# An S5 scan and an H3 convolution in one single-core kernel: parameter loads issued by ScalarE, and a written-out order of 758 operations replaced by another

## The chip, the core and the metric

The kernel runs on one core of a Trainium2 chip. A core has five engines with a queue each, which run side by side and wait for each other through semaphores: TensorE (PE; its weight loads are shown as PEld), VectorE (DVE), ScalarE (ACT), GpSimd (POOL) and SyncE (SP, which here does nothing but issue DMAs). PE writes into PSUM, which has 8 banks; ACT and DVE carry results from PSUM to SBUF ("evictions"). The metric is the device time of one execution in microseconds, as the median of several runs.

## The reference, cut to what matters

```python
# part A, columns 0..639 of the output
Lam_bar = jnp.exp(dt * Lam)                                # dt = exp(log_dt), Lam = Lambda_re + i Lambda_im
Bu = jnp.einsum("bld,pd->blp", x, ((Lam_bar - 1) / Lam)[:, None] * Bmat)
for t in range(L):                                         # L = 2048, 640 states
    h = Lam_bar * h + Bu[:, t, :]
y = 2.0 * jnp.einsum("blp,dp->bld", hseq, Cmat).real + x * Dskip
# part B, columns 640..1279
kv = causal_conv4(k, shift_k) * v                          # 4 taps along the sequence
y = irfft(rfft(kv, 4096) * rfft(ssm_k, 4096))[:2048]       # per channel
out_B = q * (y + kv * ssm_D)
```

All tensors are bf16; both parts have 2048 positions and 640 channels.

## The kernel before: how the work is staged and ordered

`build` lists some 758 operations, most of them a single engine instruction or one group of matmuls. `Program.depend` derives what each must wait for from the memory it reads and writes. `Program.emit` (L135) then issues them in the order of the string `ORDER` (L1050): `48V0` is operation 48 on DVE with bank 0. Letters are T for PE, A for ACT, V for DVE, G for POOL, S for SP. Each engine runs its own operations in this order, and an operation that waits holds everything behind it on that engine. A matmul group also waits until the operation that last read its PSUM banks is done; most groups use two banks, so four of them fit.

Part A splits the sequence into 128 blocks of 16 and builds the scan by a tree. In the code and below the operations are named so:

- `ld_par` (L346) loads Lambda and log_dt, `t_par` (L354) turns them, and a chain of small operations makes the tables (`rn`, `fr`, `fi`, `al`, `cf`, `rr`, `gm`). `ld_Braw` loads the first piece of B, `turn_B` (L499) turns it and `ev_B` (L504) evicts it; `ld_B1`, `ld_B2` (L489) and `ld_x` (L522) load by transposing DMAs.
- `up2`, `up1`, `up0` (L554, L575) are the large matmuls of the tree, evicted at L571, L595 and L620. `gC` (L544) scales C, evicted at L548. `cs_*` (L636 to L660) is the scan over the blocks: two halves h = 0, 1, each a chain of two swaps on PE (`cs_v`, `cs_k`) and six DVE operations that ends in `cs_h` (L660).
- `dn` (L677, L679) and `ad` (L695 on ACT, L697 on DVE) go down the tree. When `ad` runs on ACT, PE first adds the old value by a matmul with an identity (L677).
- `C0` to `C15` (L714) project 128 rows each, 20 matmuls; `ev_C` (L716, DVE) adds `xd` (L706) and `st_A` (L720) stores.

Part B takes two halves of 320 channels (hf = 0, 1). Its Fourier transform is done in matmul steps:

- For each of five blocks of 128 channels, `ld_k` and `ld_v` load transposed, and `cm`, `ca`, `cx` (L197 and L198, L795, L796) do the four taps. There is one buffer for k, so that `ld_k1` waits for the last `cm0`. `pl` (L802) stores the block, and `rl` (L812) reads it back in another layout.
- `ld_h` (L762) and `ld_D` (L750) load the filter of one half and its skip weight, and `addD` (L764) adds them. The filter of half 1 lands in memory that the block scan `cs_*` uses, so that its four loads wait for `cs_h` of the second half. `s1` (L832, evicted at L837) and `s2` (L850, evicted at L863) transform filter (`s1h`, `s2h`) and data (`s1k`, `s2k`). `pp`, `pq`, `py`, `pz` (L874 to L881) form the product. `r2` (L895, evicted at L900) and `r1` (L916, evicted with the factor q at L928, DVE) go back. `r1` needs the tables `g_m`, `g_q`, `g_s`, `g_k` (L324 to L333).
- `warm0` and `warm1` (L514) are four matmuls each, whose result nobody reads.

ACT computes exponentials and sines from function tables and loads another table when the kind changes. In the trace such a load carries the line of the operation behind it.

Of the kernel before, what the change touches and what calls it, by code (L numbers as in the profile page):

```python
# [20 lines left out]
PACT, PDVE, PPOOL, PPE, PSP = "A", "V", "G", "T", "S"  # L21
# [314 lines left out]
def params(c):  # L336

    P, nc, v, f = c.P, c.nc, c.v, c.f
# [4 lines left out]
    P.add("pr0", {V: .15}, lambda e: e.memset(pr, 0.0), outs=[pr])  # L343
    for k, src in enumerate((lam_re, lam_im, ldt_in)):
        rows = pr[10 * k:10 * k + 10, :]
        P.add("ld_par", {PSP: .1}, lambda e, rows=rows, src=src: e.dma_start(  # L346
            out=rows.rearrange("p (a b) -> p a b", a=2), in_=bass.AP(src.tensor, 0, [[64, 10], [0, 2], [1, 64]])),
            outs=[tk[:, k:k + 1]], ins=[pr], nbytes=2560)
    c.DR = v("DR")
# [597 lines left out]
def build(c):  # L947

    setup(c)
    params(c)  # L950
    a, b = PartA(c), PartB(c)
    c.a, c.b = a, b
# [78 lines left out]
def plain_order(P):  # L1031
# [16 lines left out]


ORDER = (  # L1050
# [36 lines left out]
)  # L1087


# [67 lines left out]
```

## Time and profile before

| | |
|---|---|
| runs | 208.45 us median of 3, 206.47 to 208.98 |
| profiled execution | span 205.6 us from first to last instruction; no other time of it is given |
| busy share of the span | PE 88%, DVE 81%, ACT 69%, POOL 37% |
| chain that ended last | PE 46%, ACT 24%, DVE 10%, DMA 10%, no wait shown 5% |
| ACT function table loads | 6 of 1.283 us |

The profile comes from one execution. In its pages a row of the timeline has the start in us, the duration, the engine (ACTq and SPq are the issue of a DMA by ACT or SP), the line, the operation, the tiles, and the count; in square brackets stands how long the engine was idle before it and what released it. `acc` is PSUM and `arena` is the one SBUF tile in which all data lie. A row of groups ends with the busy time and the mean ns of one. The view of stretches gives, for each stretch of the span, the busy time of each engine and the granted clock of PE (1.00 is full speed).

### The profile page before, as it was taken

What the parts mean: (1) busy time and instruction counts of PE and PEld (TensorE: products, weight loads), DVE (VectorE), ACT (ScalarE), POOL (GpSimd) and SP (SyncE); (2) the same over time, 40 slices, a digit from 0 to 9 for tenths busy, and PEclk for the clock granted to TensorE, in tenths of its full rate; (3) what the DMA queues carried; (4) which work ended last, traced back from release to release, by engine and by line L of the source; (5) the groups of instructions that cost most, each with busy time, mean ns of one, the idle gap of its engine ahead of it and who ended that gap; (6) DMA issues with size and microseconds to landing.
All of it is one profiled execution on the core that took longest, in us unless ns stands there. A gap on an engine that the chain in (4) does not pass through costs nothing.

```text
span 205.6 us, 8247 instructions
## 1 busy us (share of the span) xinstructions
PE 180.7 (88%) x3713; PEld 118.7 (58%) x3713; DVE 166.2 (81%) x228; ACT 142.5 (69%) x164; POOL 76.4 (37%) x63
## 2 busy tenths in 40 slices
PE   2399999999999989768759999999999998999891
PEld 0245444554556647447546757546577776887670
DVE  4929349798949698798697989999999899988821
ACT  2628897887994889999738799996999950550000
POOL 8799900000040727037310180684910507120120
PEclk9999999999999999999965899999999999999998
DMA  4999979989999989659948990140962794166866
GB/s 124 160 195 168 183 163 168 136 187 156 228 222 180 267 135 199 109 100 129 134 141 171 161 101 3 40 129 3 212 80 67 171 218 96 66 160 168 227 165 156
DMA packets 107549, 30.20 MB, mean 147 GB/s; under 512 B 102394, under 2 KB 106874, under 8 KB 107514
## 3 DMA queue, kind: packets, MB, share of 16 engines
q1 hardware_dynamic: 107226, 29.35, 77.4%
q8 instruction: 29, 0.48, 1.1%
q10 hardware_dynamic: 288, 0.33, 0.5%
q14 instruction: 6, 0.05, 0.1%
HBM read 10.99 MB, written 7.86 MB: 92 GB/s over the span
## 4 chain that ended last, share of the span: by engine, by line
PE 46%; ACT 24%; DVE 10%; DMA 10%; issue 5%; POOL 1%; SPq 0%; DVEq 0%; ACTq 0%
PE acc L714 14%; PE acc L554 12%; ACT arena L863 8%; ACT arena L837 7%; DMA arena<-in_B_k_dram 6%; PE acc L850 5%; PE acc L679 3%; PE acc L832 3%; PE acc L895 3%; DVE arena L716 2%; PE acc L575 2%; DVE arena L874 2%; ACT arena L198 2%; DVE arena L877 2%; PE acc L916 2%
## 5 line engine op out<-in xcount | busy, mean ns | idle before, releaser
L554 PE MATMUL acc<-arena 128*64 128x512 bf16 x400 | 50.0, 403 | 3.9 <-issue 3.6
L714 PE MATMUL acc<-arena 128*128 128x320 bf16 x320 | 46.0, 300 | 1.4 <-DVE arena L716 0.8
L554 PEld LDWEIGHTS <-arena 128*64 128x64 bf16 x400 | 23.4, 112 | 26.5 <-issue 6.5
L714 PEld LDWEIGHTS <-arena 128*128 128x128 bf16 x320 | 30.4, 98 | 14.4 <-issue 0.9
L837 ACT CAST arena<-acc 128x1024 bf16<-128x1024 f32 x34 | 32.7, 1033 | 5.8 <-PE acc L832 5.6
L863 ACT CAST arena<-acc 128x960 bf16<-128x960 f32 (+1 forms) x37 | 32.5, 907 | 5.7 <-PE acc L850 4.9
L850 PE MATMUL acc<-arena 128*64 128x160 bf16 x512 | 23.2, 238 | 2.5 <-ACT arena L863 1.3
L832 PE MATMUL acc<-arena 64*64 64x64 bf16 x1280 | 18.2, 205 | 6.9 <-ACT arena L837 3.0
L706 POOL TENSOR_TENSOR arena<-arena 128x640 bf16<-128x640 bf16 x9 | 13.4, 1499 | 28.0 <-DMA arena<-in_A_x_dram 28.0
L850 PEld LDWEIGHTS <-arena 128*64 128x64 bf16 x512 | 18.2, 111 | 8.8 <-ACT arena L863 3.7
L900 ACT CAST arena<-acc 128x1024 bf16<-128x1024 f32 x16 | 15.5, 1021 | 10.8 <-PE acc L895 10.8
L832 PEld LDWEIGHTS <-arena 64*64 64x64 bf16 x1280 | 14.5, 117 | 14.0 <-ACT arena L837 6.2
L795 DVE TENSOR_TENSOR arena<-arena 128x2048 bf16<-128x2048 bf16 x14 | 17.8, 1268 | 5.8 <-ACT arena L198 5.5
L198 ACT ACTIVATE arena<-arena 128x2048 bf16<-128x2048 bf16 (+3 forms) x15 | 18.6, 1243 | 5.4 <-DMA arena<-in_B_k_dram 4.2
L697 DVE TENSOR_TENSOR arena<-acc,arena 128x1024 bf16<-128x1024 f32 (+2 forms) x17 | 19.2, 1148 | 1.4 <-ACT arena L863 0.7
L881 POOL TENSOR_TENSOR arena<-arena 128x1280 bf16<-128x1280 bf16 x3 | 8.5, 2821 | 27.5 <-DVE arena L877 27.5
L716 DVE TENSOR_TENSOR arena<-acc,arena 128x640 bf16<-128x640 f32 x16 | 13.3, 832 | 4.9 <-PE acc L714 4.8
L434 POOL TENSOR_TENSOR arena<-arena 128x1280 bf16<-128x1280 bf16 x1 | 2.3, 2331 | 32.1 <-ACT arena L198 32.1
L679 PE MATMUL acc<-arena 128*128 128x512 bf16 (+2 forms) x50 | 13.0, 346 | 0.6 <-ACT arena L837 0.5
L197 DVE TENSOR_SCALAR arena<-arena 128x2048 bf16<-128x2048 bf16 (+2 forms) x17 | 11.8, 699 | 1.2 <-DMA arena<-in_B_k_dram 0.9
L928 DVE TENSOR_TENSOR arena<-acc,arena 128x960 bf16<-128x960 f32 (+1 forms) x12 | 11.9, 1040 | 0.7 <-DMA arena<-in_B_q_dram 0.4
L874 DVE TENSOR_TENSOR arena<-arena 128x2560 bf16<-128x2560 bf16 x8 | 11.9, 1486 | 0.1
(139 smaller groups left out, 269.1 us busy)
## 6 DMA issues: line engine op xcount, KB each, us to landing
out_dram<-arena SPq DMA_DIRECT2D x32, 160.0 KB, 3.1
arena<-in_B_ssm_k_dram SPq DMA_DIRECT2D x8, 320.0 KB, 7.1
kv_rows<-arena SPq DMA_DIRECT2D x5, 512.0 KB, 4.2
arena<-kv_rows SPq DMA_DIRECT2D x8, 320.0 KB, 5.6
arena<-in_A_x_dram SPq DMA_DIRECT2D x16, 160.0 KB, 4.2
arena<-in_B_q_dram SPq DMA_DIRECT2D x8, 320.0 KB, 5.7
arena<-in_A_B_im_dram ACTq DMA_DIRECT2D x1, 160.0 KB
arena<-in_A_B_re_dram ACTq DMA_DIRECT2D x1, 160.0 KB, 2.7
```

What stands on the lines that cost most here:

```text
L198: self.SM = {nc.scalar: lambda out, in_, by: nc.scalar.mul(out, in_, by), nc.vector: vm(nc.vector), nc.gpsimd: vm(nc.gpsimd)}
L554: e.matmul(o[64 * r:64 * r + 64], lhsT=self.BT[j][:, r, d, :], rhs=self.XP[:, d, 2 * q:2 * q + 2], start=(d == 0), stop=(d == 4), skip_gro ...
L679: e.matmul(B[:, o:o + 128 * k], lhsT=c.RR[:, n, j, :], rhs=A[:, j, q:q + k, 0:128], start=not by_pe, stop=True, skip_group_check=True)
L697: e.tensor_tensor(out=o, in0=b, in1=o, op=ALU.add)
L714: e.matmul(B[:, 512 * b:512 * b + 320], lhsT=lh[j], rhs=self.CT[:, j, 320 * b:320 * b + 320], start=(j == 0), stop=(j == 9))
L716: P.add(f"ev_C{i}", {PDVE: dve(640)}, lambda e, B: e.tensor_tensor(out=ys.rearrange("p (b n) -> p b n", b=2), in0=B.rearrange("p (b n) -> ...
L795: P.add(f"ca{d}_{j}", tt, lambda e: e.tensor_tensor(out=t1, in0=t1, in1=t2, op=ALU.add), outs=[t1], ins=[t1, t2])
L832: e.matmul(B[64 * b:64 * b + 64, 512 * l + 64 * i:512 * l + 64 * i + 64], lhsT=lh[i][ps], rhs=F[ps, b, :], start=True, stop=True, tile_pos ...
L837: P.add(f"e1{what}{hf}_{u}", {PACT: act(1024), PDVE: dve(1024)}, lambda e, B: c.CP[e](out=out, in_=B.rearrange("p (l n k s) -> p k s l n", ...
L850: e.matmul(B[64 * s:64 * s + 64, 512 * b + 160 * i:512 * b + 160 * i + 160], lhsT=c.W[:, k, 64 * b:64 * b + 64], rhs=self.AS[hf][:, k, 160 ...
L863: c.CP[e](out=out, in_=b.rearrange("p r (k j n) -> p r k j n", k=n, j=4) if nj > 1 else b.rearrange("p r (k x) -> p r k x", k=n))
L874: P.add(f"pp{hf}", n1, lambda e: e.tensor_tensor(out=pt, in0=X, in1=Yk, op=ALU.mult), outs=[pt], ins=[X, Yk])
```

## The change

The function of `ld_par` is on ACT instead of SP, and the whole string `ORDER` is new. No operation is added, removed or altered.

```diff
-        P.add("ld_par", {PSP: .1}, lambda e, rows=rows, src=src: e.dma_start(
+        P.add("ld_par", {PACT: .1}, lambda e, rows=rows, src=src: e.dma_start(
...
 ORDER = (
-    "48V0 33G0 50S0 123A0 51S0 115G0 122A0 108G0 42G0 49S0 6G0 72G0 7V0 73G0 137S0 1G0 18G0 0G0 30G0 2V0 119G0 8V0 114S0 12V0 465G0 "
...
-    "721V4 658T0 722S0 754V0 662T4 755T6 659V0 535S0 676S0 663V4 661V2 738S0 745T0 756V6 667S0 757S0 674S0 677S0 739G0 666S0 740T4 "
-    "665S0 746V0 747S0 664S0 120T2 741V4 742S0"
+    "114S0 48V0 72G0 42G0 115G0 33G0 6G0 18G0 73G0 83V0 8V0 9V0 12V0 122A0 7V0 27V0 25V0 136S0 0G0 11V0 19V0 26V0 269V0 1G0 2V0 "
+    "120T5 458V0 43V0 3V0 10V0 24V0 28V0 29V0 50A0 49A0 51A0 53T4 54V4 87V0 86V0 15G0 34G0 123A0 124T5 55A0 56V0 125A5 63V0 14V0 "
...
+    "664S0 739V0 740T6 741V6 742S0 744G0 745T3 746V3 747S0"
 )
```

By the names above, the two orders differ so:

| engine | before | after |
|---|---|---|
| SP, start | ld_par x3, x7, ld_sk, B1, x6, B1, k0, B2, B2, x5, x4 | ld_sk, x6, x7, B1, B1, x4, x5, B2, B2, k0 |
| ACT, start | ld_Braw, ld_Braw, dt, rn, rn, ev_B, f1_s | ld_Braw, ld_par x3, ld_Braw, dt, ev_B, rn x4, f1_s |
| PE, start | t_par, warm1, turn_B, up21_0 | warm0, t_par, turn_B, up21_0 |
| PE, around the block scan | cs_v0, 8 other groups and 6 of s2h0, cs_k0, 2 of s2h0, cs_v1, 3 of s2h0 and 3 of s1k0, cs_k1 | cs_v0, 8 other groups and 2 of s2h0, cs_k0, 2 of s2h0, cs_v1, 5 of s2h0, cs_k1, 2 of s2h0, warm1, s1k0 |
| PE, between s2k0 and s2h1 | 11 of s2k0 and C0 ahead of the first s1h1 | 7 of s2k0, dn2_0, dn2_9, dn2_5 ahead of the first s1h1; C0 after the seventh s1h1 |
| PE, end | r21 x10, C14, r11 x3, C8, r11 x3, C15, C13, C12, warm0 | C8, then r21 mixed with r10, r11 x3, C15, r11 x3, C14, C12, C13 |
| POOL | addD on DVE; 9 of xd | addD0 and addD1; 6 of xd |

91 operations have another engine: 3 `ld_par` from SP to ACT; 37 from DVE to ACT (10 evictions of 1024 columns at L571, L837 and L900, 9 at L863, 5 `ad`, 5 smaller evictions at L548 and L620, 3 taps `cm`, 3 `cf`, 2 `g_k`); 32 from ACT to DVE (13 evictions of 1024 columns, 9 at L863, 2 `ad`, 2 smaller ones, 6 taps `cm`); 8 from DVE to POOL (5 products, 2 `addD`, 1 `xd`), 9 from POOL to DVE (5 products, 4 `xd`), and 2 from POOL to ACT. By ORDER, exponentials and sines on ACT alternate so that four table loads are needed in place of six. All eight `g_k` stand on ACT (five before). `ad` stands on ACT seven times (four before). All eleven evictions of `s2h0` stand on ACT (eight before).

66 rows, old and new, of the table ORDER are left out of this document.

## The prediction

> **What bounds the kernel now.** I read the share of each engine first, then the stretches between places where PE visibly stops, then the timeline around the two longest stops.
>
> ```profile
> core 0: us, PE busy (x) PEld busy (x) DVE busy (x) ACT busy (x) POOL busy (x), PEclk, DMA share, GB/s
> 0.00:10.67 10.67, 2.96 (x16) 1.65 (x16) 7.74 (x40) 5.34 (x8) 8.39 (x24) 1.00 0.78 143
> 10.67:76.00 65.33, 64.16 (x966) 35.22 (x966) 48.20 (x69) 51.15 (x61) 21.74 (x19) 1.00 1.07 183
> 76.00:101.30 25.30, 20.36 (x633) 15.51 (x635) 22.18 (x25) 23.94 (x31) 10.25 (x5) 1.00 0.85 133
> 101.30:104.70 3.40, 0.90 (x46) 0.63 (x40) 2.27 (x3) 1.02 (x2) 2.36 (x1) 1.00 1.15 304
> 104.70:114.90 10.20, 8.88 (x313) 6.59 (x314) 9.02 (x9) 7.72 (x9) 0.00 (x0) 0.50 0.54 118
> 114.90:150.00 35.10, 33.71 (x684) 21.66 (x684) 33.10 (x35) 30.61 (x35) 21.47 (x10) 1.00 0.54 91
> 150.00:175.00 25.00, 24.23 (x420) 18.20 (x417) 23.68 (x31) 16.80 (x18) 7.38 (x4) 1.00 0.62 124
> 175.00:200.40 25.40, 24.71 (x650) 19.05 (x648) 19.18 (x21) 5.89 (x6) 4.82 (x4) 1.00 0.62 158
> ```
>
> PE is the bound from 10.67 to 76 us (64.16 of 65.33) and from 114.9 to 200.4. In 76 to 101 ACT is (23.94 of 25.30): PE waits there for evictions. Two losses remain. PE's large matmuls start only at 10.67. And PE does next to nothing from 101.3 to 104.7 (0.90 of 3.40, a share of 26%), after which its granted clock is 0.50 for the next 10.2 us.
>
> ```profile
> 102.44 1.60 DVE L764 TENSOR_TENSOR arena<-arena 128x80 bf16<-128x80 bf16 x1 [1.51 <-DMA arena<-in_B_ssm_D_dram]
> 104.13 0.44 PE L832 MATMUL acc<-arena 64*64 64x64 bf16 x32 [2.37 <-DVE arena L764]
> 89.27 0.49 DVE L660 TENSOR_TENSOR arena<-arena 128x640 bf16<-128x640 bf16 x1
> 89.91 8.05 SPq L762 DMA_DIRECT2D arena<-in_B_ssm_k_dram  x4
> 98.07 1.23 SPq L750 DMA_DIRECT2D arena<-in_B_ssm_D_dram  x1
> ```
>
> The stop at 101.3 is a chain: cs_h of the second half ends at 89.76 (L660), the four loads of half 1's filter go out from 89.91, addD1 runs at 102.44 and frees PE at 104.13. So the end of the block scan, and 12.7 us of loading behind it, set when s1h1 can begin.
>
> **The change, part by part.**
>
> *The start.*
>
> ```profile
> 0.94 0.41 SPq L346 DMA_DIRECT2D arena<-in_A_Lambda_im_dram  x1
> 1.75 0.33 SPq L346 DMA_DIRECT2D arena<-in_A_Lambda_re_dram  x1
> 2.12 1.57 SPq L522 DMA_TRANSPOSE arena<-in_A_x_dram  x1
> 3.74 0.58 SPq L745 DMA_DIRECT2D arena<-in_B_shift_k_dram  x1
> 5.74 1.80 SPq L522 DMA_TRANSPOSE arena<-in_A_x_dram  x1
> DMA to landing us min/median/max: 3.9/4.9/5.1
> 7.10 1.23 ACT L504 COPY arena<-acc 128x1280 bf16<-128x1280 bf16 x1 [0.38 <-PE acc L499]
> 10.67 1.92 PE L554 MATMUL acc<-arena 128*64 128x512 bf16 x8 [3.60 <-issue]
> ```
>
> The first large matmul waits for two pieces of x. The second is issued at 5.74 and lands 4.9 later (the landing row is that of L522), at 10.6; ev_B, its other condition, was done at 8.33. After, SP issues ld_sk (0.58) and the two pieces (1.80 and 1.57) first. From about 0.75 the second goes out at 0.75 + 0.58 + 1.80 = 3.1 and lands at 8.0. Three parameter loads and one of B leave its front. On ACT they stand ahead of the second ld_Braw and move that by their 0.94 to 2.08, 1.1 us. They themselves go out as early as on SP; but warm0 now stands ahead of t_par on PE, and its four matmuls cost t_par, dt and so ev_B some 0.2 to 0.5 us: ev_B ends near 8.5. PE starts at 8.5 in place of 10.67: **-2.2 us** (between -1.5, if warm0's input is late by 0.7, and -2.6, where x alone decides). PE has work without a pause behind it, so this carries through to 76.
>
> *The block scan and the filter of half 1.* After, four of the s2h0 groups that stood ahead of cs_k0 stand behind it, the three DVE evictions between the two halves go to ACT, and the scan no longer queues behind them. I walked the chain with the durations of the rows: cs_v0 at 70.8, cs_k0 at 76, cs_v1 at 78.1, cs_k1 at 82.8, cs_h ends near 84.6, 5 us earlier than 89.76. Loads and addD1 (on POOL, where no row shows this size: 0.2 by POOL's 1.5 for 640 columns at L706, row below, 1.6 if it runs as DVE's did) end near 98. PE reaches s1h1 near 99.5, so that the stop of 2.37 goes: -2.4. What is late next is ACT, which feeds PE in this stretch.
>
> *The half clock.* It followed a stretch of 3.4 us with PE at 26%; 76 to 101 with 20.36 of 25.30 (80%) kept clock 1.00. Without the stop I take it to stay away: of 10.2 us, 7.72 are ACT's work, so that at full clock up to 2.5 go: -2.5. By the bounds: nothing if it comes anyway, and -4.4, half of PE's 8.88, if ACT kept up.
>
> *Work moved between engines.*
>
> ```profile
> L837 ACT CAST arena<-acc 128x1024 bf16<-128x1024 f32 x34 | 32.7, 1033 | 5.8 <-PE acc L832 5.6
> L863 ACT CAST arena<-acc 128x960 bf16<-128x960 f32 x29 | 27.4, 966 | 4.1 <-PE acc L850 3.3 <-ACT arena L620 0.2
> L863 DVE CAST arena<-acc 128x960 bf16<-128x960 f32 x7 | 8.1, 1153 | 1.0 <-PE acc L850 0.5 <-ACT arena L620 0.4
> L837 DVE CAST arena<-acc 128x1024 bf16<-128x1024 f32 x6 | 7.2, 1222 | 3.9 <-PE acc L832 3.9
> L198 ACT ACTIVATE arena<-arena 128x2048 bf16<-128x2048 bf16 x6 | 12.0, 2002 | 5.2 <-DMA arena<-in_B_k_dram 4.2 <-DVE arena L795 1.0
> L197 DVE TENSOR_SCALAR arena<-arena 128x2048 bf16<-128x2048 bf16 x14 | 10.7, 768 | 1.1 <-DMA arena<-in_B_k_dram 0.9
> L877 DVE TENSOR_TENSOR arena<-arena 128x1280 bf16<-128x1280 bf16 x14 | 11.2, 821 | 0.2
> L877 POOL TENSOR_TENSOR arena<-arena 128x1280 bf16<-128x1280 bf16 x2 | 5.2, 2615 | 3.5 <-DVE arena L874 3.4
> L198 ACT ACTIVATE arena<-arena 128x1024 bf16<-128x1024 bf16 x5 | 5.7, 1154 | 0.0
> L366 ACT ACT_TABLE_LOAD x2 | 2.6, 1283 | 0.0
> L863 ACT CAST arena<-acc 128x640 bf16<-128x640 f32 x8 | 5.5, 693 | 1.7 <-PE acc L850 1.5
> L706 POOL TENSOR_TENSOR arena<-arena 128x640 bf16<-128x640 bf16 x9 | 13.4, 1499 | 28.0 <-DMA arena<-in_A_x_dram 28.0
> L900 ACT CAST arena<-acc 128x1024 bf16<-128x1024 f32 x16 | 15.5, 1021 | 10.8 <-PE acc L895 10.8
> ```
>
> Over the whole run the moves cancel. ACT gives up 13 x 1.03 and 6 x 2.0 and gets 10 x 1.03, 3 x 2.0 and a net three more `ad` (1.0) and three g_k (1.15): nil within 1 us, less two table loads (2.6). DVE gets three more evictions of 1.22 and three more taps of 0.77, and gives three `ad`, two g_k, addD and some smaller ones: 1 to 2 us less. The products change places one for one (0.82 on DVE, 2.6 on POOL). POOL loses three xd and one g_k, 6 us of time it had to spare. It is the place that counts. In 76 to 101, three s2h0 evictions come to ACT and one e1k0 leaves: 2 x 0.97 = **+1.9** on the engine that bounds. With the two terms above the middle gives -2.4 - 2.5 + 1.9 = **-3.0 us**.
>
> From 101 on ACT gets three more g_k (3.5), three more `ad` (3.0) and one table load (1.3), and hands 3 evictions of 640 columns to DVE (-2.1): some 5.7 us against the idle time it has from 101.3 to 150, which is 48.7 - 39.35 = 9.3. That hides it, barely. Two costs stay on PE. `ad` on ACT needs identity matmuls: four more of 512 columns behind s2h1, by C's 20 matmuls of 320 columns in 2.89 (row below) 0.23 each, +0.9. And the first r11 group now follows ten r21 groups, eight of whose evictions (1.02) stand on ACT, with C14 no longer between: r21 pairs leave PE faster than ACT empties them, +1.5 by my walk (0 if DVE's two finish early, 2.9 if all of C14's cover is missed). **+2.4 us.**
>
> ```profile
> 98.06 2.89 PE L714 MATMUL acc<-arena 128*128 128x320 bf16 x20
> 53.19 1.83 ACT arena L837 x2
> 55.04 1.28 ACT L452
> 56.33 1.27 ACT arena L452
> ```
>
> The table load of 1.28 begins as the eviction before it ends (53.19 + 1.83 = 55.02) and the sine follows at once. [...]
>
> DMA loads of x, C and k behind the start are covered: SP's k1 still waits for the last cm0 (DVE, about 28 as before), and k2 for cm1_0. The moved stores and r loads have 3 us or more to spare except r9 and r10, whose xd stand on DVE near 167: a miss there costs up to 1 us, and is in the range.
>
> **Sum.** -2.2 - 3.0 + 2.4 = -2.8 on a span of 205.6: 202.8. The median of the runs, 208.45, is 2.85 above the profiled span; I add that: **205.65**, said as 205.7.
>
> **Rivals.**
>
> *Nothing missed (faster).* Without the +2.4 (the idle time takes the identity matmuls, the r11 wait does not come) the sum is -5.2: 203.3. For it speaks that PE, from 114.9 on, leaves only 2.9 us unused now (85.5 less 82.65 busy) and has the same groups to run; against it, that ACT has 5.7 us more to do there than it had.
>
> *ACT takes the place (no change).* After 101 its spare 9.3 us are not in one place: where PE runs a C (2.89) ACT idles, and then cannot catch up. If half of the spare is out of reach, 5.7 - 4.7 = 1.0 more is on the path, and if none of it can be used 5.7: then -2.8 + 5.7 = +2.9 at most, 211.3; halfway 208.5. For it: g_k and er20 all precede the first r10 group. Against: 10.8 us of ACT's idle time stood among the evictions of r2 (row of L900) and can take the late g_k.
>
> *Half clock again (slower).* The new order leaves PE short pauses between groups while ACT evicts, in 84 to 101 some 60% to 65% busy by my walk, between the 26% that lost the clock and the 80% that kept it. If the clock drops there, the 10.2 us at 0.50 fall on C0 and the groups about it in full: -2.5 is not gained and C0's 2.89 doubles, -2.8 + 2.5 + 2.9 = +2.6, 211.0; if it drops once more in the PE-bound part, half of 10.2 comes on top: 216. The point from which it makes the kernel slower by 2% is a second drop. [...]
>
> *The parameter loads do nothing by themselves.* They free 1.14 us of SP; ld_B1's place between the two x's frees more. That is in the -2.2.
>
> **How the numbers follow.** The likeliest case, 202.5 to 208 by its own bounds, has 0.50; nothing missed 0.20; ACT 0.17 (208.5); half clock 0.13 (211 to 216). Within 2% of 208.45, about what a measurement of this kernel can tell from no change, lie 204.3 to 212.6. Faster: the second case and a fifth of the first, 0.30. Slower: half of the last, a little of the third and some for what I don't see, 0.12. Same: 0.58. The range, 202.3 to 211, leaves out less than 2 in 10.
>
> **What would show it.** Right: the first L554 matmul near 8.5; the second L660 near 85 and the four L762 loads at once behind it; no stop of PE over 2 us near 100; clock 1.00 from the first microseconds to the end; a pause of 1 to 2 us ahead of the first r11 group (L916). Wrong: a stretch of 0.50 in the middle; ACT without idle time from 76 to the last g_k and PE waiting for it; DVE waiting for the loads of L705.

## The result, and the profile after

| | before | changed |
|---|---|---|
| median of the runs, us | 207.64 (206.47 to 208.98, 4 runs) | 220.81 (217.71 to 221.99, 4 runs) |
| ratio, with its 95% interval | | 1.056 (1.045 to 1.067) |
| profiled execution: span, own time | 205.6, not known | 219.7, 221.48 |

The change makes the kernel 5.6% slower, some 12 us (the medians differ by 13). All ratios here are of the faster executions of either kernel, and the profiled execution of the changed one is among the longer of its four. First the stretches of its profile, cut near the places where those of before were cut.

```profile
core 0: us, PE busy (x) PEld busy (x) DVE busy (x) ACT busy (x) POOL busy (x), PEclk, DMA share, GB/s
8.92:76.00 67.08, 64.28 (x981) 34.91 (x986) 51.13 (x62) 42.98 (x65) 23.16 (x24) 1.00 1.12 186
76.00:101.30 25.30, 17.31 (x512) 12.41 (x508) 18.53 (x23) 19.77 (x24) 7.00 (x3) 0.87 0.94 112
101.30:114.90 13.60, 10.91 (x357) 8.06 (x354) 11.70 (x13) 11.31 (x14) 4.15 (x3) 1.00 0.59 123
114.90:150.00 35.10, 27.37 (x692) 17.58 (x688) 32.23 (x27) 26.79 (x29) 16.78 (x7) 0.90 0.57 107
```

From 76 to 101 both PE and ACT have idle time now (ACT 19.77 of 25.30, where it had 23.94): neither bounds. From 115 to 150 PE, the bound before (33.71 of 35.10), works 27.37; DVE has 32.23. So PE waits for something new in two places. The list of what PE waits for (us in total, times, longest) names them:

```profile
PE acc L832 <- issue: 6.0, 4, 3.1
PE acc L679 <- DVE arena L716: 4.9, 1, 4.9
...
PE acc L850 <- DVE arena L863: 1.7, 1, 1.7
PE acc L714 <- DVE arena L716: 1.5, 1, 1.5
...
PE acc L916 <- ACT arena L900: 1.1, 1, 1.1
```

The two largest were not there before: 6.0 us at the s1 groups (L832) in which PE waits for nothing that the profile shows, and 4.9 us in one piece for ev_C3 (L716). In the list of the kernel before no matmul of L679 waits for L716, and two short waits stand there, behind the start, for nothing that the profile shows:

```profile
PE acc L714 <- issue: 0.6, 1, 0.6
...
PE acc L832 <- issue: 0.3, 1, 0.3
```

The second place first, in the timelines of DVE, POOL and PE around it:

```profile
130.41 4.70 DVE L877 TENSOR_TENSOR arena<-arena 128x1280 bf16<-128x1280 bf16 x3
135.14 3.11 DVE L881 TENSOR_TENSOR arena<-arena 128x1280 bf16<-128x1280 bf16 x1
138.17 0.48 DVE L706 TENSOR_TENSOR arena<-arena 128x640 bf16<-128x640 bf16 x1
138.78 0.82 DVE L716 TENSOR_TENSOR arena<-acc,arena 128x640 bf16<-128x640 f32 x1
```

```profile
131.37 3.06 POOL L881 TENSOR_TENSOR arena<-arena 128x1280 bf16<-128x1280 bf16 x1 [1.85 <-DVE arena L877]
134.38 3.19 POOL L879 TENSOR_TENSOR arena<-arena 128x1280 bf16<-128x1280 bf16 x1
```

```profile
139.66 0.61 PE L679 MATMUL acc<-arena 128*128 128x512 bf16 x1 [4.92 <-DVE arena L716]
```

A product takes DVE 0.82. Here three of them take 4.70 and the next one 3.11: DVE's third L877 ends 0.7 us after POOL's first product does (131.37 + 3.06 = 134.43), and its L881 ends 138.25, 0.7 after POOL's second (137.57). They did not work for 3 us, they stood until POOL was done. All of it lies in front of ev_C3, whose PSUM bank dn1_6 needs.

The other place, PE's timeline near 93, where the changed order runs the s1k0 groups (32 matmuls each) one behind the other:

```profile
92.93 0.28 PE L832 MATMUL acc<-arena 64*64 64x64 bf16 x11 [0.46 <-ACT arena L837]
96.31 1.55 PE L832 MATMUL acc<-arena 64*64 64x64 bf16 x117 [3.09 <-issue]
```

PE stops for 3.09 us behind the eleventh of the 32 matmuls of s1k0_8. A wait of this program stands ahead of a group's first matmul, never inside a group.

### The profile page after: what moved, and what is told of

The parts are those of the page before. It is cut to its first block, busy times and chain, and to the rows that moved or that the text cites. A ratio compares the mean times of both kernels' runs of the same rounds, so it can differ in the third digit from the quotient of the medians.

```text
span 219.7 us, 8254 instructions
## 1 busy us (share of the span) xinstructions
PE 184.0 (84%) x3712; PEld 118.9 (54%) x3715; DVE 174.0 (79%) x224; ACT 138.8 (63%) x169; POOL 71.7 (33%) x60
## 4 chain that ended last, share of the span: by engine, by line
PE 62%; ACT 13%; DVE 13%; issue 7%; DMA 2%; ACTq 1%; DVEq 0%
PE acc L554 22%; PE acc L714 15%; ACT arena L863 7%; PE acc L850 5%; PE acc L575 4%; PE acc L832 4%; PE acc L679 4%; PE acc L895 4%; DVE arena L877 3%; ACT arena L837 3%; DVE arena L863 2%; PE acc L916 2%; DVE arena L716 2%; ACT arena L900 2%; DVE arena L881 2%
## 5 line engine op out<-in xcount | busy, mean ns | idle before, releaser
L714 PE MATMUL acc<-arena 128*128 128x320 bf16 x320 | 45.4, 299 | 2.8 <-DVE arena L716 1.5
L714 PEld LDWEIGHTS <-arena 128*128 128x128 bf16 x320 | 30.6, 98 | 15.2 <-DVE arena L716 1.6
L863 ACT CAST arena<-acc 128x960 bf16<-128x960 f32 (+1 forms) x37 | 33.2, 929 | 8.1 <-PE acc L850 7.4
L837 ACT CAST arena<-acc 128x1024 bf16<-128x1024 f32 x31 | 30.1, 1021 | 11.4 <-PE acc L832 11.4
L850 PE MATMUL acc<-arena 128*64 128x160 bf16 x512 | 24.1, 243 | 6.2 <-ACT arena L863 2.5
L850 PEld LDWEIGHTS <-arena 128*64 128x64 bf16 x512 | 19.0, 114 | 13.2 <-ACT arena L863 4.7
L900 ACT CAST arena<-acc 128x1024 bf16<-128x1024 f32 x18 | 17.8, 1016 | 12.3 <-PE acc L895 12.2
L832 PE MATMUL acc<-arena 64*64 64x64 bf16 x1280 | 16.9, 201 | 8.0 <-issue 6.0
L832 PEld LDWEIGHTS <-arena 64*64 64x64 bf16 x1280 | 13.7, 114 | 15.1 <-issue 8.5
L679 PE MATMUL acc<-arena 128*128 128x512 bf16 (+2 forms) x50 | 15.4, 390 | 5.5 <-DVE arena L716 4.9
L697 DVE TENSOR_TENSOR arena<-acc,arena 128x1024 bf16<-128x1024 f32 (+1 forms) x14 | 16.1, 1164 | 4.2 <-PE acc L679 3.2
L877 POOL TENSOR_TENSOR arena<-arena 128x1280 bf16<-128x1280 bf16 x4 | 10.4, 2612 | 27.7 <-DVE arena L874 27.7
L198 ACT ACTIVATE arena<-arena 128x1024 bf16<-128x1024 bf16 (+3 forms) x16 | 15.9, 1017 | 4.7 <-DMA arena<-in_B_k_dram 3.1
L795 DVE TENSOR_TENSOR arena<-arena 128x2048 bf16<-128x2048 bf16 x14 | 17.1, 1220 | 1.5 <-ACT arena L198 1.1
L716 DVE TENSOR_TENSOR arena<-acc,arena 128x640 bf16<-128x640 f32 x16 | 13.0, 821 | 6.6 <-PE acc L714 6.0
L197 DVE TENSOR_SCALAR arena<-arena 128x2048 bf16<-128x2048 bf16 x17 | 15.2, 905 | 0.4
L837 DVE CAST arena<-acc 128x1024 bf16<-128x1024 f32 x9 | 10.9, 1218 | 4.6 <-PE acc L832 4.5
L706 POOL TENSOR_TENSOR arena<-arena 128x640 bf16<-128x640 bf16 x6 | 8.4, 1399 | 18.4 <-DMA arena<-in_A_x_dram 18.4
L877 DVE TENSOR_TENSOR arena<-arena 128x1280 bf16<-128x1280 bf16 x12 | 13.1, 1111 | 0.2
```

Of the source, the lines that this page charges most:

```text
L679: e.matmul(B[:, o:o + 128 * k], lhsT=c.RR[:, n, j, :], rhs=A[:, j, q:q + k, 0:128], start=not by_pe, stop=True, skip_group_check=True)
L697: e.tensor_tensor(out=o, in0=b, in1=o, op=ALU.add)
L714: e.matmul(B[:, 512 * b:512 * b + 320], lhsT=lh[j], rhs=self.CT[:, j, 320 * b:320 * b + 320], start=(j == 0), stop=(j == 9))
L716: P.add(f"ev_C{i}", {PDVE: dve(640)}, lambda e, B: e.tensor_tensor(out=ys.rearrange("p (b n) -> p b n", b=2), in0=B.rearrange("p (b n) -> ...
L795: P.add(f"ca{d}_{j}", tt, lambda e: e.tensor_tensor(out=t1, in0=t1, in1=t2, op=ALU.add), outs=[t1], ins=[t1, t2])
L832: e.matmul(B[64 * b:64 * b + 64, 512 * l + 64 * i:512 * l + 64 * i + 64], lhsT=lh[i][ps], rhs=F[ps, b, :], start=True, stop=True, tile_pos ...
```

## The experiments

All ratios are to the kernel before, run beside each on the same chip; theory P is DVE standing while POOL runs, theory F is PE short of instructions, theory C is the clock.

### DVE and POOL: experiments 1, 6 and 9

**1.** The two POOL products of that timeline go to DVE.

```
-446G0 ... 456G0
+446V0 ... 456V0
```

> The changed kernel, with the two products that POOL runs between 131.4 and 137.6 us (one pz0, one py0, L881 and L879) put on DVE instead. Theory P (port): DVE's operations with all operands in the arena stand still while POOL runs a tensor operation (two of them took 3.2 and 3.1 us there instead of 0.82). Then the DVE products between 130 and 138 all take 0.82 again, ev_C3 ends near 136.4 instead of 139.61, PE's stop of 4.9 us ahead of dn1_6 shrinks to about 1.7, and the time falls by 3.2 us, by up to 2 more where the half clock behind the stop stays away: 215.5 to 217.6 against 220.8. Rival (DVE simply has too much in front of ev_C3): two more operations of 0.82 on DVE make ev_C3 later by 1.6, the stop grows to 6.5, the time is 222 or more.

Measured: 215.57 us, ratio 1.039 (1.032 to 1.046). DVE's and PE's timelines at that place:

```profile
130.40 1.56 DVE L877 TENSOR_TENSOR arena<-arena 128x1280 bf16<-128x1280 bf16 x2
132.00 0.83 DVE L881 TENSOR_TENSOR arena<-arena 128x1280 bf16<-128x1280 bf16 x1
132.74 0.82 DVE L879 TENSOR_TENSOR arena<-arena 128x1280 bf16<-128x1280 bf16 x1
133.47 0.48 DVE L706 TENSOR_TENSOR arena<-arena 128x640 bf16<-128x640 bf16 x1
134.09 0.82 DVE L716 TENSOR_TENSOR arena<-acc,arena 128x640 bf16<-128x640 f32 x1
```

```profile
134.97 0.60 PE L679 MATMUL acc<-arena 128*128 128x512 bf16 x2 [1.94 <-DVE arena L716]
```

With two more operations DVE is done earlier: every product is back to 0.82, and the stop falls from 4.92 to 1.94. Theory P holds. By the ratios 1.7% of the 5.6%, some 3.5 us, hang on these two products (the two intervals just overlap); the medians differ by 5.2.

**6.** Nearly all other clashes of that sort behind 100 us are cleared too.

```
-446G0 456G0 633G0 734G0
+446V0 456V0 633V0 734V0
-... 476G0 ... 466G0 ... (behind xd7 on POOL)
+476G0 466G0 391G0       (two g_q ahead of addD1)
```

> The changed kernel with the first experiment's edit, and the other places cleared where POOL runs beside DVE's arena operations: pz1 and xd11 go to DVE too, and two g_q of POOL stand ahead of addD1 (at 95 to 100, where DVE evicts from PSUM) instead of at 146 to 151. Theory P: the DVE operations at 141 to 144 and 180 to 187 (2.4, 1.97 and 1.9 us) fall back to 0.82 and 0.48, the PE stops of 1.8 ahead of the first s2k1 group behind them and of 1.5 ahead of C11 shrink to under 0.6, and the time falls below the first experiment's 215.6 by 2 to 3 us, to 212.5 to 213.6. Rival (DVE has too much there, or those stops are covered by the next wait): within 0.7 of 215.6.

Measured: 211.57 us, ratio 1.019 (1.013 to 1.026), somewhat better than expected. Two groups of DVE's arena-only operations (count, busy us, mean ns of one), the changed kernel first, this one second, and the second group in the kernel before last (the first, 821, stands in the prediction):

```profile
L877 DVE TENSOR_TENSOR arena<-arena 128x1280 bf16<-128x1280 bf16 x12 | 13.1, 1111 | 0.2
...
L881 DVE TENSOR_TENSOR arena<-arena 128x1280 bf16<-128x1280 bf16 x6 | 9.2, 1525 | 0.1
```

```profile
L877 DVE TENSOR_TENSOR arena<-arena 128x1280 bf16<-128x1280 bf16 x12 | 9.7, 826 | 0.2
...
L881 DVE TENSOR_TENSOR arena<-arena 128x1280 bf16<-128x1280 bf16 x8 | 7.0, 874 | 0.1
```

```profile
L881 DVE TENSOR_TENSOR arena<-arena 128x1280 bf16<-128x1280 bf16 x5 | 4.1, 820 | 0.0
```

The means are back at, or near, the 821 and 820 ns of the kernel before. The PE waits for DVE at L850 (1.7) and L714 (1.5) are gone from the list. In all, the clashes cleared here and in experiment 1 cost 3.7% (1.056 less 1.019, give or take 1.3), nearly 8 us.

**9.** On top of that, two products that still stand ahead of ev_C3 go behind the next four evictions.

```
-424V0 456V0 (ahead of 696V6, ev_C3)
+424V0 456V0 (behind 321V0, the fourth eviction after it)
```

> The kernel with POOL cleared (the sixth experiment), and on DVE the two products pz0 and py0 that still stand ahead of ev_C3 put behind the next four evictions. Theory P (all that held ev_C3 was DVE's queue): ev_C3 ends within 0.9 us of the end of C3, the stop of 1.93 ahead of dn1_6 and the half clock behind it go, and the time falls by 1.5 to 2 us from 211.6 to 209.6 to 210.1. What then stays against the kernel before, 2 us or so, is no more than the stop inside s1k0 (2.95) and the smaller fetch stops. Rival (the products are late next, and r2 waits for them): 211 or more.

Measured: 212.51 us, ratio 1.025 (1.019 to 1.031): no gain, the rival is right. The stop ahead of dn1_6 is gone, and one of 2.39 stands further on instead, where s2k1's evictions wait on DVE behind the moved products:

```profile
141.93 0.88 PE L850 MATMUL acc<-arena 128*64 128x160 bf16 x20 [2.39 <-DVE arena L863]
```

DVE's queue is full there; what is moved out of one wait's way stands in the next one's.

### PE's instructions: experiments 2, 3, 5, 12 and 13

The page's list of DMA queues has, besides the data, this one (packets, MB, share):

```profile
q8 instruction: 29, 0.48, 1.0%
```

29 packets with 0.48 MB are 16 KB each; PE issues 3712 matmuls and 3715 weight loads, so one packet is 7427 / 29 = 256 instructions, 128 matmuls. In the trace's DMA records (start, duration, number of the matmul that PE had reached, and how many since the packet before) four are of interest:

```
changed   84.29  1.24  #1115
          93.06  1.64  #1365  +250   <- PE stopped at #1365 until 96.31
before    87.92  0.93  #1278
          91.81  1.20  #1444  +166
          95.78  1.34  #1528  +84
```

In the changed kernel no packet comes for 250 matmuls, and there PE stops; a stop of this sort is called a fetch stop below. The filter loads (L762) are being issued from 87.67 to 95.59. The other stops inside groups, 0.98 (55 us), 1.20 (68), 0.60 and 0.72 (107 and 111), 0.91 and 1.28 (behind 195), make 8.8 us with this one. Behind each of the seven PE goes on 1.3 to 1.6 us after a packet has ended. The kernel before has two such stops, 0.26 and 0.61, 0.9 us in all (the rows "issue" of its list above; the 1.9 in an expectation below is not in that list).

**3.** 32 more matmuls ahead of s1k0 in the same time.

```
-            for _ in range(4):                                  # 512 columns each
+            for _ in range(36 if k else 4):                     # 64 columns each in warm1
```

> The changed kernel, with the four matmuls of 512 columns of warm1 (at 87.7 us, 0.73 us) replaced by 36 of 64 columns that take about as long: 32 more matmuls stand ahead of s1k0 in PE's stream, and nothing else changes. Theory F: the instruction blocks end 32 matmuls earlier in the program, so the long stop without a semaphore comes 32 matmuls earlier, behind about the 16th matmul of s1k0_4 and no longer in s1k0_8, and again in the middle of a group; the fetches lie 128 matmuls apart on average as before. Rival (a wait in s1k0_8): the stop stays behind the eleventh matmul of s1k0_8. Time within 2 us of 220.8 by both.

Measured: 218.91 us (one run). PE's timeline (the edit moves the line numbers behind it by one, that of experiment 2 by two):

```profile
88.16 0.58 PE L833 MATMUL acc<-arena 64*64 64x64 bf16 x48 [0.20 <-ACT arena L838]
91.03 0.32 PE L833 MATMUL acc<-arena 64*64 64x64 bf16 x16 [2.29 <-issue]
...
95.58 0.53 PE L833 MATMUL acc<-arena 64*64 64x64 bf16 x21 [2.01 <-issue]
```

The 48 matmuls are s1k0_3 and half of s1k0_4: the stop comes behind the sixteenth matmul of s1k0_4, as theory F has it, which is matmul #1365 of PE's stream again, and a second one stands exactly 128 later (#1493). The place belongs to the stream, not to a group.

**5.** The filter loads wait for the last s1k0 group.

```
-... 390S0 ...                        (behind 380A2, in ORDER)
+... 390S0 ...                        (behind 369T0, s1k0_1)
+    c.P.ops[390].preds.add(369)      # ld_h1 behind s1k0_1
```

> The changed kernel, with half 1's filter loads held back until PE has run the last s1k0 group (one wait added to the first of them): they go out near 94 instead of 87.7 and land some 6 us later. Theory F (PE's next instructions come late because they queue behind these loads): the fetch that started at 93.06 goes out at 90 to 91, the stop inside s1k0_8 falls under 0.6 us and no half clock follows it; in exchange PE waits 3 to 6 us for the late filter ahead of s1h1_3 (addD1, L764). Rival (the fetch is late whatever the loads do, because s1k0's small matmuls eat a block faster than any fetch comes): the stop stays at 2 to 3 us. The total says little by either, 217 to 223.

Measured: 222.72 us, ratio 1.059 (1.049 to 1.070). In the trace the packets now start at 84.34, 90.00 and 93.49. PE's timeline, and its waits:

```profile
91.58 0.28 PE L832 MATMUL acc<-arena 64*64 64x64 bf16 x11 [0.46 <-ACT arena L837]
92.35 1.20 PE L832 MATMUL acc<-arena 64*64 64x64 bf16 x117 [0.48 <-issue]
```

```profile
PE acc L832 <- POOL arena L764: 7.6, 1, 7.6
```

The same eleven matmuls, and 0.48 in place of 3.09: the packet was late because of those loads. The price is a wait of 7.6 for the filter (expected: 3 to 6), and the time is that of the changed kernel (1.059 against 1.056).

**2.** The same bytes of the filter in long runs.

```
+            if hf:
+                src = bass.AP(c.ins["B_ssm_k"].tensor, 2048 * c0, [[5120, 32], [64, 80], [1, 64]])
```

> The changed kernel, with half 1's four filter loads (L762) reading as many bytes from the same rows in long runs instead of pieces of 128 bytes (half 1's filter is then in another order, so part B's second half computes with permuted filter values). Theory F (fetch): the stop of 3.09 us after the eleventh of the 32 matmuls of s1k0_8, which waits for no semaphore, is PE waiting for its next 16 KB of instructions; that fetch went out only at 93.06, 250 matmuls after the one before it, queued behind the small pieces of these loads. With long runs the stop falls under 1 us, the half clock that follows at 96.8 stays away, and the time falls by 2.5 to 4.5 us, to 216.3 to 218.3. Rival (PE waits there for an eviction that the profile doesn't show as a wait): the stop stays at 2.5 to 3.5 us, and the time within 1 us of 220.8.

Measured: 217.38 us, ratio 1.045 (1.036 to 1.053), but not for the reason expected: the stop grew, and the packet started at 93.67, 2.2 us behind the eleventh matmul's end; in experiment 5 it started 1.9 ahead of it.

```profile
91.20 0.28 PE L834 MATMUL acc<-arena 64*64 64x64 bf16 x11 [0.46 <-ACT arena L839]
96.26 0.48 PE L834 MATMUL acc<-arena 64*64 64x64 bf16 x19 [4.78 <-issue]
```

So the small pieces are not what held this packet up: with long runs PE stopped for 4.78 in place of 3.09. That it stood behind the bytes already queued would explain both, but that is a guess: no run separates bytes from pieces further. The interval overlaps that of the change (1.045 to 1.067), so the gain of the whole is not shown either.

**12 and 13.** The s1 groups in half as many instructions, on the kernel of experiment 6 and, as a control, on the kernel before.

```
-            for i in range(8):
+            for i in range(0, 8, 2):
...
-                        e.matmul(B[..., 512 * l + 64 * i:512 * l + 64 * i + 64], lhsT=lh[i][ps], rhs=F[ps, b, :], ...)
+                        e.matmul(B[..., 512 * l + 64 * i:512 * l + 64 * i + 128], lhsT=lh[i][ps], rhs=c.F1[ps, 0:128], ...)
```

> The kernel with POOL cleared (the sixth experiment), with every s1 group (L832) run in 16 matmuls of 128 columns in place of 32 of 64: as many columns through PE, half the instructions. It computes other values (each matmul uses one weight for both halves), so the outputs of part B are not the reference's. Theory F: the stops without a semaphore at s1 groups (2.95 near 93, 1.27 near 55, 0.72 near 110) fall under 0.5 each, and the time falls by 3 to 5 us from 211.6 to 206.6 to 208.6, level with the kernel before. Rival (other waits stand right behind these stops): 210.5 or more.

> The kernel before, with the same halving of the s1 groups, as a control: what fewer instructions are worth where s1 hardly stops (its stops without a semaphore are 0.26 to 0.61 us, 1.9 in all). Theory F: it gains 0 to 1.2 us, 206.5 to 207.7 against 207.7. Rival (half the instructions speed s1 up by themselves, fetch or not): it gains 3 us or more, as the changed kernel does.

Measured: 206.42 us, ratio 0.993 (0.990 to 0.997), from 1.019; the control 205.55, ratio 0.988 (0.982 to 0.995). PE's timeline of the first, where s1k0 runs (32 of its matmuls are two groups):

```profile
88.32 0.64 PE L832 MATMUL acc<-arena 64*64 64x128 bf16 x32 [0.46 <-ACT arena L837]
89.24 0.65 PE L832 MATMUL acc<-arena 64*64 64x128 bf16 x32 [0.27 <-ACT arena L837]
```

No s1 group stops inside any more, the gaps left are waits for ACT; stops inside groups are 2.1 us in all, from 9.1 in experiment 6 (control: 0.5, from 0.9). The gain is 2.6% of before's time (5.3 us); the control gains 1.2% (2.4 us), more than theory F expected and less than its rival. So the fetch stops that the change added are worth the difference, 1.4% or some 3 us (give or take 2); the other 2.4 us are what half as many instructions give the kernel before too.

### The clock: experiments 4 and 7

**4 and 7.** Idle matmuls in the long stop, of the changed kernel (18) and of the one before (10).

```
+    a.warm(2)                        # 18 (10) matmuls of 512 columns, nobody reads them
+758T0 306T6                          # ahead of dn1_6   (before: 758T6 502T6, ahead of s1h1_9)
```

> The changed kernel, with 18 idle matmuls of 512 columns (about 3.9 us, their result is used by nothing) put on PE in the stop of 4.9 us ahead of dn1_6, from about 135.3 to 139.2. The stop in PE's useful work stays, only PE's activity changes. Theory C (the half clock behind the stops is a cost of its own): the clock stays at 1.00 between 137.8 and 144.6, and the time falls by 2 to 3.4 us, half of PE's work in that stretch. Rival (behind the stop ACT and DVE set the pace, and PE's clock is hidden): the clock stays at 1.00 too, and the time within 0.7 us of 220.8.

> The kernel before, with 10 idle matmuls of 512 columns (2.1 us, used by nothing) in its stop of 2.37 us at 101.8 to 104.1, so that PE stays active there and the clock should stay at 1.00 through 104.7 to 114.9. The prediction's price of that half clock: -2.5 us, 205.6 against 208.1, at most -4.4. Rival (from the experiment with the filler in the changed kernel, where a kept clock gave nothing): within 0.7 of 208.1, since DVE and ACT set the pace there.

Measured: 220.44 us, ratio 1.062 (1.055 to 1.069), against 1.056 for the change without them; and 207.47, ratio 0.996 (0.991 to 1.000). The clock stayed up behind the filler in both, as the stretches show: first the changed kernel without it and experiment 4, then experiment 7 (where it was 0.50 in the second row without the filler).

```profile
137.77:144.60 6.83, 4.93 (x134) 2.31 (x134) 5.57 (x7) 2.94 (x3) 0.00 (x0) 0.50 0.21 57
```

```profile
136.00:144.60 8.60, 7.42 (x198) 4.12 (x196) 8.35 (x8) 6.49 (x8) 3.35 (x2) 1.00 0.68 119
```

```profile
101.30:104.70 3.40, 3.35 (x62) 1.78 (x62) 2.38 (x2) 0.96 (x1) 2.61 (x1) 1.00 1.24 135
104.70:114.90 10.20, 8.22 (x351) 6.05 (x338) 10.06 (x11) 9.40 (x11) 0.00 (x0) 1.00 0.79 186
```

The rival is right both times: DVE sets the pace behind the filler (8.35 of 8.60 in experiment 4; 10.06 of 10.20 in experiment 7, with ACT at 9.40), and PE's clock hardly matters. By the interval the half clock of the kernel before was worth 0 to 0.9%, 1.8 us at most and 0.9 by the ratio, where I had put 2.5. In both profiles the clock fell elsewhere instead (0.50 from 91.39 to 98.22 in experiment 4, from 90.65 to 94.06 in experiment 7), so these are bounds more than prices.

### The start: experiments 8, 10, 11, 14 and 15

**8 and 15** (the same kernel twice), **14** (the reverse) and **11** (the parameter loads alone).

```
8, 15: kernel before, ld_par (50, 49, 51) on ACT between 122 and 123; SP: 114 136 137 126 127 first
14:    changed kernel, ld_par on SP; SP: 50 51 49 137 114 127 136 126 first; ACT: 123 122
11:    kernel before, ld_par on ACT between 123 and 122; SP as it was without them
```

> The kernel before, with the start of the changed one: the parameter loads on ScalarE between the two pieces of B, and on SP the small load and the two pieces of x first. The prediction's step: the first large matmul starts 1.7 to 2.2 us earlier and PE carries this through to 76, -1.7 to -2.2: 206 to 206.4 against 208.1. Rival (PE is not alone the bound behind the start: evictions, loads of k and v and the block scan keep their times): the start is earlier by as much, and the time within 0.7 of 208.1.

> The kernel before with the three parameter loads on ScalarE, between its two pieces of B, and nothing else changed. By the prediction they free 1.14 us of SP ahead of x: x7 and x6 go out 1.1 to 1.2 earlier, the first large matmul starts near 9.5 instead of 10.6, and the time falls by 0.5 to 1.2: 206.5 to 207.2 against 207.7. Rival (the start is set by the B pieces, of which the second leaves ScalarE 1.1 later, or the lead is lost again behind it): within 0.4 of 207.7.

> The changed kernel, with the start of the kernel before: parameter loads on SP, then x7, the small load, a piece of B and x6. By the prediction's step (the lead at the start carries through) it is 1.5 to 2.2 us slower than the changed kernel: 222.3 to 223 against 220.8. Rival (the fetch stops at s1h0, which lie in this stretch, and the block scan's chain take the lead away): within 0.7 of 220.8.

> The kernel before with the changed start, a second time, beside the reverse of it: the first time it gave 206.5 against 207.7, and with one more edit 208.0. If the lead at the start reaches the end, 206 to 206.6 again; if not, 207.3 to 208.

| | first large matmul, us | time, us | ratio |
|---|---|---|---|
| 8: before, changed start | 9.73 | 206.49 | 0.989 (0.983 to 0.995) |
| 15: the same again | 9.68 | 207.11 | 0.995 (0.991 to 0.999) |
| 11: before, parameter loads alone | 9.51 | 207.86 | 1.002 (0.998 to 1.006) |
| 14: changed kernel, old start | 10.64 | 220.50 | 1.063 (1.057 to 1.070) |

PE starts a microsecond earlier with the parameter loads alone, and the time does not change. In the changed kernel the old start costs 1.7 us at the start and nothing at the end: the first product of the block scan (L649) begins at 73.66 in the changed kernel, and with the old start no later:

```profile
73.50 0.82 DVE L649 TENSOR_TENSOR arena<-acc,arena 128x640 bf16<-128x640 f32 x1
```

In the kernel before, the whole changed start is worth 0.5% and 1.1% (0.1% to 1.7% by the intervals); of the parts tried it is the one that beats the kernel before, and by little.

**10.** That kernel, with the one POOL product beside addD1 on DVE.

```
-423G0 (behind 391V0, addD1)
+423V0 (ahead of it)
```

> The kernel before with the changed start, and with its one py0 on POOL at 101.1 to 103.7 put on DVE ahead of addD1, where DVE waits 1.5 us for a load anyway. Theory P: addD1 (1.60 us there, beside POOL's product) takes about 0.53, PE's stop of 2.38 falls to about 1.3, and the time falls by 0.5 to 1.1 from 206.5: 205.4 to 206. Rival (addD1 waits for its load and not for POOL): 206.5 within 0.4.

Measured: 208.01 us, ratio 1.001 (0.996 to 1.005): no gain. What was to change did: addD1 takes 0.52 in place of 1.70 (experiment 8 first, this one second), and the stop behind it is 0.56 in place of 2.38.

```profile
101.62 1.70 DVE L764 TENSOR_TENSOR arena<-arena 128x80 bf16<-128x80 bf16 x1 [1.41 <-DMA arena<-in_B_ssm_D_dram]
```

```profile
101.79 0.52 DVE L764 TENSOR_TENSOR arena<-arena 128x80 bf16<-128x80 bf16 x1
```

```profile
102.41 0.45 PE L832 MATMUL acc<-arena 64*64 64x64 bf16 x32 [0.56 <-issue]
106.32 0.22 PE L832 MATMUL acc<-arena 64*64 64x64 bf16 x3 [0.94 <-issue]
```

A longer fetch stop (0.94, it was 0.26 in experiment 8) follows, but it need not come from the edit: experiment 15, the same kernel as 8, has 1.17 at that place. Where the gain went is open. The run also shows the clash in the kernel before: addD1's 1.60 in the prediction's first rows was DVE standing beside py0 on POOL, whose row there is

```profile
101.06 2.60 POOL L879 TENSOR_TENSOR arena<-arena 128x1280 bf16<-128x1280 bf16 x1 [4.53 <-ACT arena L863]
```

## Why the prediction was wrong, step by step

- **The start** was right at its place (8.92 in the changed kernel, 8.5 predicted) and wrong in "carries through to 76". Up to 76 PE stood 2.80 us (67.08 less 64.28), 1.6 more than before (65.33 less 64.16); two fetch stops inside s1h0 groups stand there, 0.98 and 1.20. Experiment 14 shows that nothing of the lead is left at 73.5; with the old start one stop of 1.33 is left of the two, so they account for 0.9 of the 1.7 that are lost, and the rest is open.
- **Block scan and filter of half 1**: the order of events was right, 3 us late. cs_h ends at 87.6 (84.6 predicted, 89.76 before), the loads follow at once, addD1 runs on POOL at 100.59 in 0.90. The stop of 2.37 ahead of s1h1 is gone; PE reaches s1h1 at 105.5, not 99.5; 3.6 of the 6 us are fetch stops that now lie ahead of it (3.09, and 0.55 at 100.9), and the rest was not taken apart. "What is late next is ACT" was wrong: it is PE's own instructions, and ACT has 5.5 us to spare in that stretch.
- **The half clock** was wrong twice. It did not stay away: it came four times, each behind a window of 3.4 us in which PE was half busy or less,

```profile
79.74:83.16 3.42, 1.71 (x38) 1.25 (x36) 3.35 (x5) 3.32 (x4) 0.00 (x0) 1.00 0.99 167
93.40:96.81 3.41, 0.50 (x59) 0.51 (x61) 0.02 (x2) 0.40 (x1) 1.99 (x1) 1.00 1.18 112
134.36:137.77 3.41, 0.39 (x44) 0.28 (x32) 3.38 (x2) 1.82 (x2) 3.21 (x2) 1.00 0.02 5
148.01:151.42 3.41, 1.49 (x39) 1.14 (x36) 3.41 (x4) 1.90 (x3) 2.90 (x2) 1.00 0.48 134
```

  and it would have been worth 0.9 us, 1.8 at most, not 2.5 (experiment 7). The rival *half clock again* had the sign, and many drops, but not the cause: the drops follow the stops, and experiment 4 shows no gain from taking the longest of them away.
- **Moves between engines** is the step that failed worst: "the products change places one for one (0.82 on DVE, 2.6 on POOL)" and "over the whole run the moves cancel". Each operation was costed by its own duration. POOL's time was not spare time, though: the DVE product that began at 131.87, 0.5 us into one of POOL's that took 3.06, ended after 3.24 in place of 0.82. Which operations meet is set by the order, and in the new one nine of DVE's are longer than their like beside a POOL operation, by 12 us together; in the old one there are four behind the start, by 2.3. Experiments 1 and 6 put nearly 8 us on this, where the prediction's sum had nothing. The row that should have told me stood in the prediction: addD1 at 1.60 us beside a POOL product; I priced addD1's move by it and did not ask why 80 columns take DVE 1.60.

  Not every operation beside POOL was longer. In the changed kernel the product that began at 131.14, ahead of POOL's, took its 0.82; the tap at 42.23 (L795), begun while POOL ran L324, took its 1.22; and DVE's operations of 960 and 1024 columns that read PSUM took 1.14 to 1.23 beside POOL, as they do without it.
- **Behind s2h1**: the pause ahead of the first r11 group came as forecast (1.1, from 1.5). It was not tried alone.
- **What no step had**: PE's instruction stream. The new order runs the s1k0 groups faster, while the filter loads go out: PE uses 128 matmuls' worth of instructions in 2.9 us (90.3 to 93.2; the kernel before took 3.75 for 128 there, 90.57 to 94.32). The next packet starts 2.8 us after PE began on them (93.06), where it started 1.2 after in the kernel before (91.81) and 1.05 after with the loads held back (experiment 5), and PE goes on at 96.31. Experiments 3 and 5 show the cause of the stop, and 12 with its control 13 puts some 3 us on all such stops that the change added. Before had small signs of it: 0.9 us of stops inside groups. The trace has one packet for 256 instructions (7427 in 29), and PE stood up to 3.09 us for one of them.

Clashes (3.7%) and the instruction fetch that the change added (1.4%: 2.6 less the control's 1.2) are 5.1% together, of the 5.6% of the result; each is known to about 1%, so no third cause is needed, and a small one is not excluded.

## What to carry to other kernels

When an order moves work between DVE and POOL, list which arena-only operations of DVE will run at the same time as a POOL operation, and cost each that begins behind POOL's at POOL's remaining time (here 3.24 us for the product at 131.87, 2.56 of them until POOL's ended). When small matmuls are brought together, count instructions per microsecond as well as columns, and look at which loads are in the DMA queues when the next packet of instructions is due (here a stop of 3.09 us with the filter loads in the queues, 0.48 with them held back). And before a half clock or an earlier start is given a price, find the engine that sets the pace in that stretch: if it isn't PE, the price is small: under 1% for the half clock and 0.5% to 1.1% for the start here.

## What the runs showed of the hardware that I had not expected

- A stop inside a group, at matmuls a multiple of 128 apart (#1365, #1493 with 32 matmuls added ahead; #602, #858 and #1365 in the changed kernel, a few records missing), is PE waiting for 16 KB of instructions: up to 3.09 us in the changed kernel, and 4.78 with long runs in the queue.
- After such a stop PE went on 1.3 to 1.6 us after the packet had ended (93.06 + 1.64 = 94.70, next matmul 96.31).
- In the changed kernel, five of DVE's products of 1280 columns that began while a POOL operation ran ended 0.7 us after it (1.27 to 3.24 us, where one takes 0.82 alone), and two of POOL's own were longer too (3.06 and 3.19 in place of 2.61).
- The clock of the changed kernel fell behind windows with PE busy 50% (1.71 of 3.42) and less, that of experiment 7 once behind one of 57% whose pauses were all under 0.5 us (1.93 of 3.41, from 87.24); at 26% in the kernel before it stayed at 0.50 for 10.2 us, here for 3.4 or 6.8.
